# A fused attention and MLP block on one core: tile 0's value product in two column halves, tile 1's statistics on ScalarE, w2 loaded in two parts, and a new order of the work

## The chip, the core and the metric

The kernel runs on one core of a Trainium2 chip. The core has TensorE (PE, matrix products), VectorE (DVE), ScalarE (ACT), GpSimd (POOL) and SyncE (SP), which here only issues transfers; 16 DMA engines carry these. The metric is the device time of one execution in microseconds (us).

## The reference

The input x has 2048 tokens of 448 features. Two branches work on the same layernorm of x and are added to it:

```python
xn = _layernorm(x)
return x + _A_ref(xn, wqkv, w_phi, wo) + _B_ref(xn, w1, w2, w3, w4)

# _A_ref: linear attention, 16 heads of 28
pq = einsum("bhsd,hdf->bhsf", q, w_phi); pk = the same of k
phi_q = concat([softmax(pq), softmax(-pq)]); phi_k = the same of pk
kv = einsum("bhsf,bhsd->bhfd", phi_k, v); z = sum of phi_k over tokens
o = einsum(phi_q, kv) / (einsum(phi_q, z) + 1e-6); return o @ wo

# _B_ref: a mixer and an MLP
h = gelu(_layernorm(xn) @ w1)
hs = (four column groups of h, shifted by +1, -1, +2, -2 tokens) @ w2
x1 = xn + hs
return x1 + gelu(_layernorm(x1) @ w3) @ w4
```

## The kernel before, in words

The tokens are 16 tiles of 128 (NT = 16). Weights and activations are bf16, products accumulate in the 8 PSUM banks (`banks`). A class `Recorder` (lines 19 to 222) takes every operation in program order, works out which semaphore waits the data need, and plays each engine's list in that order; so the order of the Python calls is the order of every engine and of every DMA queue. Its helpers `mm` (L204), `tr` (L208), `act` (L212), `ew` (L216), `dma_t` (L219) and `dma` (L222) are the lines that the profile names.

TensorE is used as two halves of 64 rows that run at the same time: LO (rows 0 to 63) and HI (rows 64 to 127). The contraction over 448 features lies in four overlapping blocks of 128 (`lap`), so that a product is seven matmuls of 64 rows: four on one half and three on the other.

Two lists set the order. `chain([...], 400, "1001...")` plays the first stage; each entry makes a job:

- `HD` dummy products that keep TensorE busy; `L(("m", i))` the statistics of tile i on VectorE (`bn_stats`, `bn_aggr`, into `mv`); `("q", i, 1)` the reciprocal root on ScalarE and `("r", i, 1)` on GpSimd (into `rs`); `("a", i)` applies the layernorm on VectorE, `("p", i)` on GpSimd, into `xn`.
- `XT(i, ...)` transposes tile i on TensorE and copies it to `xnT`; `XD(i)` does it by a DMA transpose on SyncE.
- `ZV(i, EV(...))` the value product of tile i and its copy to `vaug`; `ZW`, `ZH` the product with w1 (whole, or 256 columns) and its gelu to `hT`; `ZR` the last 64 features of it (`rest_out` to gT, then `rest_T`, the DMA transpose hRT<-gT); `FO` folds w_phi into the weights of q and k (casts to `wpk`, `wpq`).
- `do(h_shift, g)` six DMA copies hT<-hT, which bring the shifted column groups to where the w2 product reads them with the HI rows (the LO rows read `hT` directly); `do(load_w2)`, `do(load_w3, h)` weight loads. All of these stand in SyncE's queue.
- `HF(p, n)` half n of the first head pair: p = 0 the first w2 product (tiles 0 and 1, reads `w2`, `hT` and `hRT`), p = 1 the k product, p = 2 the q product.

The string gives, for each "zip" job, which half takes four of the seven matmuls; 400 is the distance, in columns, that `chain` keeps between the halves' work on one bank. `vb` and `gb` name the PSUM bank of each value and w1 product. The second list, `play([...])`, orders the rest: k and q products and their exponentials (`k0`, `q0`), w2 products (`w0`, `w1_`), the second layernorm (`lo`, `sc`, `A` on GpSimd, `AD` on VectorE), k's norm (`kn`, `kx`), the sums over tokens (`K`), w3 and w4 products (`a`, `b`, `f`), the attention output (`N`) and stores (`S`).

Of the kernel before, what the change touches and what calls it, by code (L numbers as in the profile page):

```python
# [12 lines left out]
LN_EPS = 1e-5  # L13
# [211 lines left out]
def bass_parallel_sum__linear_kernel_hedgehog__mixer_s_mlp__prompt_kernel(  # L225
# [17 lines left out]
    with es:  # L243
# [172 lines left out]
        R.ew(pool, "memset", st[:, :, 8:9], D * LN_EPS)  # L416
        R.ew(dve, "memset", vp[:, :, DH + 1:VP], 0.0)
# [457 lines left out]
        def ln1(*ops):  # L875
            for op, *n in ops:
                if callable(op):
                    op()
                elif op == "m":
                    ln_stats(st, mv, xtok, *n)  # L880
                elif op == "r":
                    ln_scale(mv, rs, *n)
                elif op == "q":
                    ln_root(*n)
                elif op == "v":
                    ln_var(st, mv, *n)
                else:
                    ln1_apply(pool if op == "p" else dve, *n)
# [47 lines left out]
        def HF(p, n):  # L936
# [4 lines left out]
        vb = {0: 6, 1: 7, 2: 5, 3: 0, 4: 6, 5: 5, 6: 1, 7: 1, 8: 0, 9: 7, 10: 6, 11: 2, 12: 7, 13: 7, 14: 5, 15: 2}  # L941
        gb = ((4, 2, 3), (7, 6, 4), (3, 0, 5), (0, 5, 6))
        spin(30)
        chain([
            HD(1, 3), HD(3, 3), do(load_wT, 0, (1, 2, 3)), HD(2, 3), L(("m", 1)), L(("q", 1, 1)), L(("m", 0)),
            L(("q", 0, 1)), HD(3, 3), L(("a", 1)), L(("p", 0)), HD(5, 3), XT(1, 2, 1, "ACT"), HD(0, 3), L(("m", 2)),
            L(("m", 3)), XT(0, 2, 1, "ACT"), L(("q", 3, 1)), L(("r", 2, 1)), L(("m", 4)), L(("a", 3)), L(("q", 4, 1)),
            L(("m", 5)), ZV(1, EV(1, "ACT", 1)), ZV(0, EV(0, "ACT", 1)), L(("p", 2)), XT(2, 4, 1, "ACT"),
            inside(1, ZH(1, 0), XT(3, 0, 1, "ACT")), L(("m", 7)), L(("r", 5, 1)), L(("a", 4)), L(("p", 5)),
            L(("q", 7, 1)), L(("m", 6)), L(("r", 6, 1)), ZH(2, 0), L(("a", 7)), ZV(2, EV(2, "ACT", 1)),  # L950
            inside(1, ZH(0, 0), XT(4, 0, 1, "ACT")), L(("p", 6)), inside(2, ZH(0, 1, EW(0, 0, 1)), XT(5, 6, 1, "2")),
            L(("m", 15)), inside(1, ZH(2, 1), XT(7, 0, 1, "2")), L(("q", 15, 1)), L(("p", 15)),
            ZV(4, EV(4, "ACT", 1)), L(("m", 14)), inside(2, ZH(1, 1, EW(0, 1, 2)), XT(6, 0, 1, "DVE")), L(("m", 12)),
            ZV(5, EV(5, "ACT", 1)), L(("r", 14, 1)), L(("m", 13)), L(("p", 14)), ZV(6, EV(6, "ACT", 1)), L(("m", 11)),
            ZW(1, 0, EW(1, 0, 1)), ZW(1, 1, EW(1, 1, 1)), ZW(1, 2, EW(1, 2, 1)), L(("m", 10)), L(("r", 13, 1)),
            L(("r", 12, 1)), XT(14, 2, 2, "ACT"), L(("a", 12)), L(("r", 11, 1)), ZV(7, EV(7, "DVE", 1)), L(("a", 13)),
            L(("m", 8)), L(("p", 11)), ZV(3, EV(3, "ACT", 1)), ZV(15, EV(15, "ACT", 1)), XT(12, 6, 1, "2"),
            do(kv_picks), XT(13, 3, 1, "2"), do(phi_blocks), L(("r", 10, 1)), L(("r", 8, 1)), XD(11),
            L(("a", 10)), XD(10), ZV(14, EV(14, "ACT", 1)), L(("m", 9)), L(("p", 8)), ZV(12, EV(12, "DVE", 1)),
            ZW(3, 0, EW(3, 0, 1)), XT(8, 3, 1, "ACT"), FO(1, 2, 0), do(h_shift, 0), L(("r", 9, 1)),  # L960
            ZW(3, 2, EW(3, 2, 1)), FO(1, 0, 0), FO(1, 2, 1), ZV(13, EV(13, "ACT", 1)), ZW(3, 1, EW(3, 1, 1)),
            FO(1, 0, 1), L(("p", 9)), ZV(8, EV(8, "DVE", 1)),
            inside(3, ZR(0, 6, (rest_out, 0, 6), (rest_T, 0)), XT(9, 1, 1, "DVE")), FO(0, 0, 0), FO(0, 2, 0),
            ZR(1, 7, (rest_out, 1, 7)), do(load_w2), FO(0, 0, 1), ZW(2, 2, EW(2, 2, 1)), ZW(2, 1, EW(2, 1, 1)),
            FO(0, 2, 1), do(load_w3, 0), ZV(10, EV(10, "ACT", 1)), ZW(2, 0, EW(2, 0, 1)), do(rest_T, 1),
            ZV(9, EV(9, "ACT", 1)), ZV(11, EV(11, "DVE", 1)), HF(1, 0), HF(0, 0), HF(2, 0), HF(1, 1), do(late_3), do(kv_ones),
            HF(0, 1), HF(2, 1), do(h_shift, 1)], 400,
            "100100110101110000101010011110100")
# [62 lines left out]
        def wo_in(eng="SP"):  # L1031
# [4 lines left out]
            (lo, 1), (load_w3, 1), (k0, 1), (w0, 2), (lo, 0), (kn, 0), (k1, 1), (q0, 1), (w1_, 2), (q1, 1), (T, 0),  # L1036
            (k0, 2), (q0, 2), (k1, 2), (q1, 2), (k0, 3), (q0, 3), (T, 1), (kn, 1), (T, 3), (k1, 3), (w0, 4), (q1, 3),
            (kx, 0), (kn, 2), (T, 2), (kx, 1), (w1_, 4), (kn, 3), (k0, 4), (T, 5), (w0, 6), (k1, 4), (lo, 3), (kx, 2),
            (q0, 4), (lo, 2), (w1_, 6), (q1, 4), (kn, 4), (k0, 5), (kx, 3), (k0, 6), (sc, 0), (k1, 5), (w0, 8),
            (wo_in,), (q0, 5), (A, 0), (w1_, 8), (k1, 6), (T, 6), (AD, 1), (T, 4), (q0, 6), (kn, 5), (T, 7), (q1, 5),  # L1040
            (w0, 10), (load_w4, 0), (A, 3), (k0, 7), (A, 2), (w1_, 10), (q1, 6), (lo, 5), (lo, 6), (w0, 12), (k1, 7),
            (q0, 7), (G, 0), (K, 0), (kx, 4), (K, 1), (G, 1), (kx, 5), (lo, 7), (lo, 4), (G, 2), (K, 3), (K, 4),
            (G, 3), (sc, 4), (K, 6), (A, 7), (kn, 6), (K, 9), (q1, 7), (load_w4, 1), (A, 6), (A, 4), (w1_, 12),
            (K, 8), (K, 5), (K, 7), (lo, 10), (A, 5), (K, 11), (K, 2), (kx, 6), (G, 4), (kn, 7), (G, 7), (K, 10),
            (a, 0), (lo, 11), (kx, 7), (a, 1), (G, 6), (b, 0), (lo, 12), (b, 1), (w0, 14), (a, 2), (lo, 8), (a, 3),
# [48 lines left out]
```

## Time and profile before

| | before |
|---|---|
| runs | 170.62, 171.19, 171.85 us (median 171.19) |
| profiled execution | 171.11 us, of which the span of the trace is 169.4 us |
| TensorE busy | 165.0 us, 97% of the span, 2355 matmuls |
| VectorE, ScalarE, GpSimd busy | 109.9, 79.6 and 92.4 us |
| granted TensorE clock | 1.00 of full speed |
| chain that ended last | TensorE 86%, SyncE's queue 4%, DMA 4%, VectorE 3% |

A row of a timeline has the start in us, the duration in us, the engine (PE matmuls, PEld weight loads, SPq transfers being issued by SyncE), the line, the operation with its output and inputs, and in brackets the idle time ahead of it and what ended that. A row of busy time by stretch has the stretch, its length, the busy time of PE, PEld, DVE, ACT and POOL with the number of instructions in brackets, the granted clock, the share of the DMA engines and GB/s. The chain has start, duration, and what the time went to. A row of DMA issues has the count, the size of each and the median us from issue to landing.

### The profile page before, as it was taken

To read this page: it belongs to the slowest core of one execution; us is meant where nothing else is said; L and a number is where in the kernel's file an instruction comes from. 1 tells how busy PE (TensorE), PEld (TensorE's weight loads), DVE (VectorE), ACT (ScalarE), POOL (GpSimd) and SP (SyncE) were. 2 spreads that over 40 slices of the span, in tenths; PEclk is the share of its full clock that TensorE was granted. 3 is DMA by queue.
4 is the path that set the end of the run, shared out by engine and by line. 5 is a ranking of instruction groups with operands and counts; after the bars stand their busy time and mean duration, and the time that the engine had idled before them with its cause. 6 is when DMAs were issued, how large, how long until landed. Compare 5 with 4: busy or idle time off the path is not lost.

```text
span 169.4 us, 5416 instructions
## 1 busy us (share of the span) xinstructions
PE 165.0 (97%) x2355; PEld 99.2 (59%) x2355; DVE 109.9 (65%) x247; ACT 79.6 (47%) x107; POOL 92.4 (55%) x126
## 2 busy tenths in 40 slices
PE   8899999999999999999999999999999999999994
PEld 7476678666888775535554555545555555544453
DVE  2899777269999999995885836755755252560031
ACT  3489964849998787455242420440140222224000
POOL 5569872002999999994455684162362724252040
DMA  5995443799999976459785159363133112013021
GB/s 146 356 217 105 75 90 85 144 294 270 194 117 240 241 102 191 68 112 130 165 110 107 24 108 154 77 106 63 32 66 85 35 54 62 0 31 99 17 81 54
DMA packets 50583, 19.93 MB, mean 118 GB/s; under 512 B 41728, under 2 KB 49856, under 8 KB 50560
## 3 DMA queue, kind: packets, MB, share of 16 engines
q1 hardware_dynamic: 49440, 18.71, 55.1%
q10 hardware_dynamic: 1120, 0.89, 1.6%
q8 instruction: 18, 0.29, 0.8%
q14 instruction: 5, 0.04, 0.1%
HBM read 7.14 MB, written 1.84 MB: 53 GB/s over the span
## 4 chain that ended last, share of the span: by engine, by line
PE 86%; SPq 4%; DMA 4%; DVE 3%; POOL 1%; issue 1%
PE banks L204 85%; SPq L222 4%; DMA xtok<-in_A_x_dram 2%; DMA hRT<-gT 2%; DVE st L216 1%; PE banks L208 1%; DVE vaug L216 1%; POOL rs L216 1%; DVE mv L216 0%; POOL xn L216 0%; DVE xn L216 0%; SPq L219 0%
## 5 line engine op out<-in xcount | busy, mean ns | idle before, releaser
L212 ACT ACTIVATE phik<-banks 128x1024 bf16<-128x1024 f32 (+1 forms) x44 | 41.6, 987 | 63.5 <-PE banks L204 63.5
L204 PE MATMUL banks<-gT,w 64*128 64x512 bf16 x392 | 47.1, 376 | 0.1
L216 DVE TENSOR_TENSOR vaug<-banks,vaug 128x464 f32<-128x464 f32 (+3 forms) x65 | 32.8, 514 | 20.5 <-PE banks L204 18.8
L204 PE MATMUL banks<-w,phik 64*128 64x448 bf16 (+3 forms) x434 | 45.2, 343 | 0.0
L216 POOL TENSOR_TENSOR xnT<-vaug 128x280 bf16<-128x280 f32 (+1 forms) x32 | 18.1, 588 | 35.6 <-DVE vaug L216 35.6
L721 POOL TENSOR_TENSOR phik<-phik,rks 128x1792 bf16<-128x1792 bf16 x8 | 25.6, 3215 | 15.3 <-DVE rks L216 15.3
L204 PEld LDWEIGHTS banks<-w,phik 64*128 64x128 bf16 (+1 forms) x434 | 22.3, 94 | 19.5 <-issue 0.4
L204 PE MATMUL banks<-wv,xnT 64*128 64x448 bf16 (+2 forms) x222 | 33.0, 346 | 0.1
L204 PEld LDWEIGHTS banks<-gT,w 64*128 64x128 bf16 x392 | 18.3, 94 | 19.5 <-ACT phik L212 1.4
L216 POOL TENSOR_TENSOR vaug<-xn,xtok 128x448 f32<-128x448 bf16 x16 | 16.2, 1032 | 9.1 <-DVE vaug L216 9.1
L204 PEld LDWEIGHTS banks<-wv,xnT 64*128 64x128 bf16 (+1 forms) x222 | 13.7, 94 | 9.0 <-ACT xnT L212 0.8
L216 DVE RECIPROCAL vaug<-banks 128x16 f32<-128x16 f32 x16 | 4.1, 257 | 21.6 <-PE banks L204 21.6
L204 PE MATMUL banks<-xnT,w 64*128 64x512 bf16 (+1 forms) x105 | 17.6, 334 | 0.0
L216 DVE TENSOR_REDUCE ksum<-phik 128x64 f32<-128x1792 bf16 x8 | 16.0, 1997 | 0.2 <-ACT phik L212 0.2
L204 PE MATMUL banks<-wpk,xnT 64*128 64x448 bf16 x112 | 15.4, 349 | 0.0
L204 PE MATMUL banks<-wpq,xnT 64*128 64x448 bf16 x112 | 15.1, 349 | 0.0
L212 ACT ACTIVATE hi<-banks 128x896 bf16<-128x896 f32 x16 | 13.9, 937 | 1.2 <-PE banks L204 1.2
L204 PE MATMUL banks<-w,hT 64*128 64x448 bf16 x96 | 14.0, 349 | 0.0
L216 POOL TENSOR_TENSOR rs<-mv,mhalf 128x1 f32<-128x1 f32 (+1 forms) x14 | 9.6, 690 | 2.6 <-DVE mv L216 2.4
L216 POOL TENSOR_SCALAR g_tok<-xn,rs 128x512 bf16<-128x512 bf16 x12 | 9.2, 775 | 2.9 <-DMA gT<-g_tok 2.6
L204 PEld LDWEIGHTS banks<-wpk,xnT 64*128 64x128 bf16 x112 | 8.7, 94 | 2.6 <-ACT phik L212 0.2
L216 DVE BATCH_NORM_STATS2 st<-xtok 128x6 f32<-128x448 bf16 x16 | 9.7, 604 | 0.7 <-DMA xtok<-in_A_x_dram 0.7
(63 smaller groups left out, 167.2 us busy)
## 6 DMA issues: line engine op xcount, KB each, us to landing
w<-in_B_w_dram SPq DMA_DIRECT2D x2, 896.0 KB, 5.5
out_dram<-vaug SPq DMA_DIRECT2D x15, 112.0 KB, 1.9
w<-in_B_w_dram SPq DMA_DIRECT2D x2, 784.0 KB, 5.6
xtok<-in_A_x_dram SPq DMA_DIRECT2D x2, 448.0 KB, 6.5
wv<-in_A_wo_dram SPq DMA_DIRECT2D x2, 224.0 KB, 3.7
xtok<-in_A_x_dram SPq DMA_DIRECT2D x3, 112.0 KB, 4.0
xtok<-in_A_x_dram ACTq DMA_DIRECT2D x3, 112.0 KB, 4.2
w<-in_B_w_dram SPq DMA_DIRECT2D x1, 336.0 KB, 4.3
```

The source lines that it names most:

```text
L204: self.op("PE", lambda e: e.matmul(out, lhsT, rhs, start=start, stop=stop, skip_group_check=True), [out], [lhsT, rhs], tile=self._tile(lhsT))
L208: self.op("PE", lambda e: e.transpose(out, in_, ident), [out], [in_, ident], tile=self._tile(in_))
L212: self.op("ACT", lambda e: e.activation(out, in_, func, **kw), [out], [in_] + aps)
L216: self.op(eng, lambda e: getattr(e, name)(out, *args, **kw), [out], aps)
L222: self.op(eng, lambda e: e.dma_start(out, in_), [out], [in_], dma=True)
L721: R.op(pool, lambda e: e.tensor_tensor(ph, ph, wide, op=ALU.mult), [ph], [ph, wide, *after])
```

## The change

Four things are changed; what is computed stays.

1. The value product of tile 0 is made by `HC(0, 0)` and `HC(0, 1)`: two column halves of 224 in banks 0 and 1, of which LO begins with the first and HI with the second, and then they cross over. It is 14 matmuls of 224 columns instead of 7 of 448, and `EC` copies both banks with one ScalarE instruction.
2. The statistics of tile 1 come from ScalarE: `act_sum` runs twice over the tile (a copy scaled by -1/448 with an accumulated output, which is minus the mean, and a square with that as bias, whose accumulated output is the sum of squares), and `act_root` takes the root. VectorE loses one `bn_stats` and one `bn_aggr`, GpSimd gets a memset of the epsilon and applies tile 1.
3. `load_w2` is in two parts: first the two pieces of 64 rows, then the large piece.
4. Both lists, the string and the bank tables are new.

```diff
-        def load_w2(eng="SP"):
-            R.dma(w2[:, 0:NH, :], B_w2[0:REST, :].rearrange("(m p) d -> p m d", p=128), eng)
-            for h in range(2):
-                R.dma(w2[64 * h:64 * h + 64, NH, :], B_w2[REST:D, :], eng)
+        def load_w2(h, eng="SP"):
+            if h:
+                for k in range(2):
+                    R.dma(w2[64 * k:64 * k + 64, NH, :], B_w2[REST:D, :], eng)
+            else:
+                R.dma(w2[:, 0:NH, :], B_w2[0:REST, :].rearrange("(m p) d -> p m d", p=128), eng)
...
+        R.ew(pool, "memset", st[:, 1, 0:1], LN_EPS)
...
-            m, op = (mvt[:, i, 0:1], ALU.subtract) if eng == dve else (rst[:, i, 1:2], ALU.add)
+            m, op = (mvt[:, i, 0:1], ALU.subtract) if eng == dve and (mvt is mv2 or i != 1) else (rst[:, i, 1:2], ALU.add)
...
+        def act_sum(i, sq):
+            t, o = xn[:, NT - 1 - sq, 0:D], mv[:, i, 1:2] if sq else rs[:, i, 1:2]
+            m = rs[:, i, 1:2]
+            if sq:
+                R.op("ACT", lambda e: e.activation(t, xtok[:, i, :], ACT.Square, bias=m, accum_out=o), [t, o],
+                     [xtok[:, i, :], m])
+            else:
+                R.op("ACT", lambda e: e.activation(t, xtok[:, i, :], ACT.Copy, scale=-1.0 / D, accum_out=o), [t, o],
+                     [xtok[:, i, :]])
+
+        def act_root(i):
+            R.act(rs[:, i, 0:1], mv[:, i, 1:2], ACT.Abs_reciprocal_sqrt, scale=1.0 / D, bias=st[:, i, 0:1])
...
-            if eng == pool:
+            if eng == pool and i != 1:
                 ln_neg(mv, rs, i, 1)
...
+        def HC(i, n, *then):
+            v = lap_pair([banks[vb[i] + k][:, 0:D // 2] for k in range(2)],
+                         lambda k, kc, lo, hi: xnT[lo:hi, kc, 128 * i:128 * i + 128],
+                         lambda k, kc, lo, hi: wv[lo:hi, kc, D // 2 * k:D // 2 * k + D // 2], False)
+            return "both", halves_of(*v[n], n == 0), then
+
+        def EC(i):
+            vd = vaug[:, i, :].rearrange("p (b h e) -> p b h e", b=2, e=VP)[:, :, :, 0:DH]
+            vs = two(vb[i])[:, :, 0:D // 2].rearrange("p b (h e) -> p b h e", e=DH)
+            return R.act, vd, vs, ACT.Copy
...
-            HD(1, 3), HD(3, 3), do(load_wT, 0, (1, 2, 3)), HD(2, 3), L(("m", 1)), L(("q", 1, 1)), L(("m", 0)),
...
+            HD(3, 3), L(("m", 0)), HD(0, 3), L(("s", 1, 0)), HD(2, 3), L(("q", 0, 1)), L(("s", 1, 1)), L(("t", 1)),
...
-            ZR(1, 7, (rest_out, 1, 7)), do(load_w2), FO(0, 0, 1), ZW(2, 2, EW(2, 2, 1)), ZW(2, 1, EW(2, 1, 1)),
...
+            XD(10), do(load_w2, 1), FO(1, 2, 1), ZW(3, 1, EW(3, 1, 1)), L(("p", 9)), do(load_w2, 0), do(h_shift, 0),
...
```

What this makes of SyncE's queue between the last weight transposes (hi<-in_A_wqkv) and w3, first before (x6 and the like mean that so many equal rows follow one another; xnT<-xn are `XD(11)` and `XD(10)`, the hT<-hT rows `h_shift(0)`, the first hRT<-gT `rest_T(0)`):

```order
L219 DMA_TRANSPOSE xnT<-xn 128x4x128 x2
L222 DMA hT<-hT 48x1024
L222 DMA hT<-hT 32x1023
L222 DMA hT<-hT 16x1024
L222 DMA hT<-hT 16x1023
L222 DMA hT<-hT 32x1024
L222 DMA hT<-hT 48x1022
L222 DMA w2<-in_B_w2_dram 128x3x448
L222 DMA w2<-in_B_w2_dram 64x448 x2
L219 DMA_TRANSPOSE hRT<-gT 128x4x128
L222 DMA w3<-in_B_w3_dram 128x2x1792
```

and after:

```order
L219 DMA_TRANSPOSE xnT<-xn 128x4x128 x2
L222 DMA w2<-in_B_w2_dram 64x448 x2
L222 DMA w2<-in_B_w2_dram 128x3x448
L222 DMA hT<-hT 48x1024
L222 DMA hT<-hT 32x1023
L222 DMA hT<-hT 16x1024
L222 DMA hT<-hT 16x1023
L222 DMA hT<-hT 32x1024
L222 DMA hT<-hT 48x1022
L219 DMA_TRANSPOSE hRT<-gT 128x4x128
L222 DMA w3<-in_B_w3_dram 128x2x1792
```

The three loads of w2 have moved ahead of the six shift copies; hRT<-gT follows all nine in both.

VectorE's list around the apply of tile 10 (TENSOR_SCALAR xn<-xtok,mv,rs), which the second xnT<-xn transpose reads; before:

```order
L216 CAST vaug<-banks 128x16x28
L216 COPY xnT<-banks 128x4x64
L216 MEMSET pick 32x1 x4
L216 COPY xnT<-banks 128x4x64
L216 TENSOR_TENSOR g_tok<-g_tok,maskb 112x448
L216 TENSOR_SCALAR xn<-xtok,mv,rs 128x512
```

and after, where the first TENSOR_SCALAR is tile 11 and the second tile 10:

```order
L216 TENSOR_SCALAR xn<-xtok,mv,rs 128x512
L216 CAST vaug<-banks 128x16x28
L216 TENSOR_SCALAR xn<-xtok,mv,rs 128x512
L216 TENSOR_TENSOR g_tok<-g_tok,maskb 112x448
L216 CAST vaug<-banks 128x16x28
```

Tile 10's apply now stands ahead of the masking of g_tok, and the copies and memsets have gone behind it; tile 11's apply has come from GpSimd.

TensorE's first products, before (L208 rows are transposes of a tile, eight each; 128x448 and 128x256 are a matmul's columns; `wv,xnT` is a value product, `xnT,w1` a w1 product):

```order
L208 MATMUL banks<-ident,xn 128x64 x8
L204 MATMUL banks<-const-bfloat16-1.0 128x128 x6
L208 MATMUL banks<-ident,xn 128x64 x8
L204 MATMUL banks<-wv,xnT 128x448 x10
L208 MATMUL banks<-ident,xn 128x64 x8
L204 MATMUL banks<-xnT,w1 128x256
```

and after:

```order
L208 MATMUL banks<-ident,xn 128x64 x8
L204 MATMUL banks<-const-bfloat16-1.0 128x128 x6
L208 MATMUL banks<-ident,xn 128x64 x8
L204 MATMUL banks<-wv,xnT 128x224 x14
L204 MATMUL banks<-wv,xnT 128x448 x3
L208 MATMUL banks<-ident,xn 128x64 x8
L204 MATMUL banks<-xnT,w1 128x256
```

Ten matmuls of 448 columns ahead of tile 2's transposes have become fourteen of 224 and three of 448. The first transposes are of tile 1 before and of tile 0 after.

More of the change, by code (lines that the diff above doesn't have):

```diff
@@ new lines, in bass_parallel_sum__linear_kernel_hedgehog__mixer_s_mlp__prompt_kernel @@
+            ZV(2, EV(2, "ACT", 1)), L(("m", 6)), L(("r", 6, 1)), L(("a", 7)), inside(1, ZH(0, 0), XT(4, 0, 1, "ACT")),
+            inside(2, ZH(0, 1, EW(0, 0, 1)), XT(5, 6, 1, "2")), inside(1, ZH(2, 1), XT(7, 0, 1, "ACT")), L(("m", 14)),
+            L(("p", 6)), do(load_wT, 0, (1, 2, 3)), L(("r", 14, 1)), L(("m", 15)), L(("p", 14)),
+            ZV(4, EV(4, "DVE", 1)), inside(2, ZH(1, 1, EW(0, 1, 2)), XT(6, 0, 1, "DVE")), L(("m", 12)),
+            ZV(5, EV(5, "ACT", 1)), L(("r", 15, 1)), L(("r", 12, 1)), ZW(1, 2, EW(1, 2, 1)), L(("p", 12)),
@@ new lines, in bass_parallel_sum__linear_kernel_hedgehog__mixer_s_mlp__prompt_kernel @@
+            ZW(1, 1, EW(1, 1, 1)), ZV(3, EV(3, "ACT", 1)), L(("a", 15)), L(("m", 13)), XT(14, 2, 2, "ACT"),
+            L(("m", 11)), L(("m", 9)), L(("r", 13, 1)), L(("m", 8)), ZW(1, 0, EW(1, 0, 1)), L(("m", 10)),
+            L(("p", 13)), L(("r", 11, 1)), ZV(6, EV(6, "DVE", 1)), L(("a", 11)), ZV(14, EV(14, "ACT", 1)),
+            L(("r", 8, 1)), ZV(15, EV(15, "DVE", 1)), XD(11), L(("r", 10, 1)), L(("a", 10)), XT(12, 6, 1, "ACT"),
+            do(phi_blocks), XT(13, 3, 1, "ACT"), L(("p", 8)), ZV(7, EV(7, "ACT", 1)), ZV(12, EV(12, "DVE", 1)),
@@ new lines, in bass_parallel_sum__linear_kernel_hedgehog__mixer_s_mlp__prompt_kernel @@
+            L(("r", 9, 1)), ZW(3, 0, EW(3, 0, 1)), XT(8, 4, 1, "2"), ZW(3, 2, EW(3, 2, 1)), FO(1, 2, 0), FO(1, 0, 0),
+            XD(10), do(load_w2, 1), FO(1, 2, 1), ZW(3, 1, EW(3, 1, 1)), L(("p", 9)), do(load_w2, 0), do(h_shift, 0),
+            FO(1, 0, 1), ZV(13, EV(13, "ACT", 1)), ZV(8, EV(8, "ACT", 1)),
+            inside(3, ZR(0, 6, (rest_out, 0, 6), (rest_T, 0)), XT(9, 3, 1, "DVE")), do(late_3), FO(0, 2, 0),
+            FO(0, 0, 0), ZW(2, 0, EW(2, 0, 1)), ZW(2, 2, EW(2, 2, 1)), ZW(2, 1, EW(2, 1, 1)), do(kv_ones),
@@ L970, in bass_parallel_sum__linear_kernel_hedgehog__mixer_s_mlp__prompt_kernel @@
+            FO(0, 2, 1), ZV(9, EV(9, "ACT", 1)), do(kv_picks), ZV(11, EV(11, "ACT", 1)), do(load_w3, 0), FO(0, 0, 1),
+            ZR(1, 1, (rest_out, 1, 1)), ZV(10, EV(10, "DVE", 1)), HF(1, 0), HF(0, 0), do(rest_T, 1), do(h_shift, 1),
+            HF(2, 0), HF(1, 1), HF(0, 1), HF(2, 1)], 400,
+            "11101010111001010001010011110010")
         kp = [phi_pair(wpk, 2 * n, kq[n][0]) for n in range(8)]
@@ L1041, in bass_parallel_sum__linear_kernel_hedgehog__mixer_s_mlp__prompt_kernel @@
[L1041 to L1045, printed above, removed]
```

79 lines of the change are left out of this document (34 added, 45 removed).

## The prediction

> **What bounds the kernel now.** I read the page first, then busy time by stretch, then the chain of waits in order of time, then the timelines of single engines at the places that the chain names. The page's first line and the stretches say where time can be won at all:
>
> ```profile
> PE 165.0 (97%) x2355; PEld 99.2 (59%) x2355; DVE 109.9 (65%) x247; ACT 79.6 (47%) x107; POOL 92.4 (55%) x126
> ```
> ```profile
> 4.00:8.00 4.00, 3.19 (x61) 1.90 (x61) 3.45 (x11) 1.69 (x5) 2.06 (x5) 1.00 1.08 353
> 8.00:12.00 4.00, 3.91 (x82) 2.69 (x78) 3.63 (x12) 3.08 (x9) 2.73 (x6) 1.00 1.64 273
> 32.00:36.00 4.00, 3.77 (x40) 2.09 (x41) 0.85 (x5) 2.40 (x3) 0.00 (x0) 1.00 0.80 223
> ```
>
> TensorE is the bound, at full granted clock (the 1.00 behind the counts). Its matmul work is the same after the change (below), so a new order can only remove idle TensorE time, and there is little: after 8 us only the stretch from 32 us is visibly short. The chain names what ended last in the first third:
>
> ```profile
> 1.71 4.04 DMA xtok<-in_A_x_dram
> 5.77 0.64 DVE st L216
> 10.50 0.78 POOL xn L216
> 11.33 0.29 PE banks L208 x8
> 27.01 0.59 SPq L222
> 30.12 2.72 DMA hRT<-gT
> 32.97 32.65 PE banks L204 x513
> 65.72 101.35 PE banks L204 x1269
> ```
>
> Up to 5.77 us the kernel waits for x; around 11 us for a normalized tile; then for SyncE's queue and the transpose hRT<-gT, up to 32.97; from there TensorE runs through. So two places can change: the start and the first w2 product.
>
> **The change, part by part.** Term 1, the first w2 product. SyncE's queue and TensorE there:
>
> ```profile
> 19.52 3.49 SPq L219 DMA_TRANSPOSE xnT<-xn  x2
> 23.06 4.55 SPq L222 DMA_DIRECT2D hT<-hT  x6
> 27.65 2.43 SPq L222 DMA_DIRECT2D w<-in_B_w_dram  x3
> 30.12 1.27 SPq L219 DMA_TRANSPOSE hRT<-gT  x1
> ```
> ```profile
> 21.36 1.66 SPq L219 DMA_TRANSPOSE xnT<-xn  x1
> ```
> ```profile
> 20.92 0.41 DVE L216 TENSOR_SCALAR xn<-xtok,mv,rs 128x512 bf16<-128x512 bf16 x1
> ```
> ```profile
> 31.96 0.09 PEld L204 LDWEIGHTS banks<-w,hT 64*128 64x128 bf16 x1 [0.26 <-DMA w<-in_B_w_dram]
> ```
> ```profile
> 31.97 0.36 PE L204 MATMUL banks<-w,hT 64*128 64x448 bf16 x1
> 32.17 0.35 PE L204 MATMUL banks<-w,hT 64*128 64x448 bf16 x1
> 32.20 0.35 PE L204 MATMUL banks<-wv,xnT 64*128 64x448 bf16 x1
> 32.36 0.35 PE L204 MATMUL banks<-w,hT 64*128 64x448 bf16 x1
> 32.40 0.35 PE L204 MATMUL banks<-wv,xnT 64*128 64x448 bf16 x1
> 32.97 0.35 PE L204 MATMUL banks<-w,hRT 64*128 64x448 bf16 x1 [0.23 <-DMA hRT<-gT]
> 32.98 0.36 PE L204 MATMUL banks<-wv,xnT 64*128 64x448 bf16 x1
> ```
>
> Each row half of TensorE starts a 448-column product every 0.19 to 0.20 us (31.97, 32.17, 32.36). The next on the first half, which reads hRT, comes at 32.97 instead of 32.36 + 0.19 = 32.55: 0.42 us lost. The other half loses as much (32.40 to 32.98, less 0.19 = 0.39), since its product stands behind the waiting one. The first weights of w2 cost a wait too: 0.26 us of no weight load, of which the first half feels some and the other half, busy with the value product, none; I count at most 0.14. In all about 0.4 to 0.5 us; the bounds are 0.23 (both halves idle, the row at 32.97) and 0.42 + 0.26 = 0.68 (all of both).
>
> The change issues w2's three transfers ahead of the six shift copies. The queue is in order and all ten instructions stay, so the hRT transpose still follows six copies and three loads; what moves it is that the second xnT<-xn transpose no longer waits. The first, at hRT's 1.27, ends at 19.52 + 1.27 = 20.79; the second begins at 21.36, when VectorE has just made xn[10] (20.92 + 0.41 = 21.33): 0.58 us idle. After the change that apply stands earlier in VectorE's list, ahead of the masking of g_tok, the copies of xnT and four memsets that are before it now; by my walk through the list it is done at 20.2 to 20.4 us, ahead of 20.79. So hRT is issued at 30.12 - 0.58 = 29.54 and lands, with the same 2.72, at 32.26. TensorE wants it at about 32.4 to 32.5 (the 32.55 above, less what it did not lose on w2). Then the wait is gone: -0.44 us. If xn[10] comes later than 20.79, hRT follows one for one; above 0.4 us late nothing of the gain is left.
>
> What is late next: the shift copies, now behind 448 KB of w2. The sixth was issued at 27.01 and must be so at 27.01 + 2.43 + 0.04 - 0.58 = 28.90. It is read only by the other half's third w2 product, 0.77 us behind the hRT product's place (first one below, then 0.19 each), so near 33.3 us. That leaves 4.4 us to land.
>
> ```profile
> 33.37 0.35 PE L204 MATMUL banks<-w,hT 64*128 64x448 bf16 x1
> ```
> ```profile
> w<-in_B_w_dram SPq DMA_DIRECT2D x1, 336.0 KB, 4.3
> hT<-hT SPq DMA_DIRECT2D x2, 32.0 KB, 3.8
> hT<-hT SPq DMA_DIRECT2D x1, 95.9 KB, 5.5
> hT<-hT SPq DMA_DIRECT2D x1, 31.9 KB, 5.2
> ```
>
> Shift copies took 3.8 to 5.5 us from issue to landing; most are under 4.4, so I cost this at nothing and keep 5.5 - 4.4 = 1.1 us for the range. w2 itself, issued from about 22.5 us, needs 4.3 us and is read near 31.9: covered by 5 us.
>
> Term 2, the start. TensorE's early work and what holds it:
>
> ```profile
> 3.52 0.63 DVE L216 BATCH_NORM_STATS2 st<-xtok 128x6 f32<-128x448 bf16 x1 [0.38 <-DMA xtok<-in_A_x_dram]
> 5.77 0.63 DVE L216 BATCH_NORM_STATS2 st<-xtok 128x6 f32<-128x448 bf16 x1 [0.31 <-DMA xtok<-in_A_x_dram]
> ```
> ```profile
> 6.71 0.57 POOL L216 TENSOR_TENSOR rs<-mv,mhalf 128x1 f32<-128x1 f32 x1
> 7.66 0.77 POOL L216 TENSOR_SCALAR xn<-xtok,rs 128x512 bf16<-128x512 bf16 x1
> ```
> ```profile
> 8.48 0.17 PEld L208 LDWEIGHTS banks<-ident,xn 64*128 64x128 bf16 x8 [0.38 <-POOL xn L216]
> ```
> ```profile
> 6.75 1.80 PE L204 MATMUL banks<-wv,xnT 64*128 64x448 bf16 x10
> ```
> ```profile
> 4.47 0.20 ACT L212 ACTIVATE rs<-mv 128x1 f32<-128x1 f32 x1 [2.40 <-DVE mv L216]
> 9.79 0.55 ACT L212 ACTIVATE vaug<-banks 128x448 bf16<-128x448 f32 x1
> ```
>
> Before the transposes of tile 2 at 8.48 TensorE has only tiles 0 and 1: ten value products of 448 columns from 6.75. The change puts fourteen of 224 (seven times 448) and three of 448 there: the same columns, also ten. And tile 2 hangs on its own x (5.77), its statistics, and POOL's three steps from 6.71 to 7.66 + 0.77 = 8.43, which the change leaves. Whatever tiles 0 and 1 win ends in that wait. VectorE's freed 0.63 (and an aggregate of 0.2) falls in its idle time ahead of 5.77. The two passes of tile 1's statistics on ScalarE have no row; the nearest is 0.55 for 128x448, so 1.1 us, 1.5 if each cost the 0.20 of a 128x1 more. From 3.5 us with tile 0's root (0.20) between, they end at 4.9 to 5.3; POOL, which applied tile 0 ahead of it, applies tile 1 by 6.1, still before it is wanted at 6.71. Nothing, then; twice the upper price would push POOL by 1 us and with it tile 2 (+0.5). The Trainium skill (ScalarE: Activation LUTs, What ACT_TABLE_LOAD costs) gives an ACTIVATE 186 ns + 0.833 ns per element, and 93 ns for each pointer operand. By it the two are an estimated 0.56 + 0.65 = 1.2 us; the same page's Rules for kernel authors give such arithmetic to VectorE, and if tile 1 were what TensorE waits for, the move would by these figures cost 1.2 - 0.8 = 0.4 us and the sum be 171.1. The trace agrees on the durations (0.63 and an aggregate against about 1.1) and not on the cost, since ScalarE idles 2.40 us ahead of 4.47.
>
> Past 8.5 us the later gates move by tenths both ways: tile 5's transposes waited for POOL until 11.33 (the chain's row) and now come an apply earlier, but tile 7's copy is whole on ScalarE, 0.60 instead of 0.38, ahead of tile 6's. I take -0.05, bounds -0.3 and +0.3.
>
> Term 3, all else: more second-layernorm applies on VectorE (65% busy) and fewer on POOL, wo's loads earlier, w4's halves swapped. The chain's longest rows are TensorE alone (32.65 + 101.35 us), and the moved consumers keep at least 0.2 us by my walk: 0, bounds -0.2 and +0.5.
>
> Sum: -0.44 - 0.05 + 0 = -0.5 us. The profiled execution took 171.11 us (span 169.4, 1.7 around it), 0.08 under the median of the runs shown. I forecast 170.7 us.
>
> **Rivals.** A: no gain, 171.1. The hRT transpose moves 0.58 at most and needs about 0.4 of it; xn[10] 0.4 late, a slower transpose (the second hRT transpose took 6.4 us, row below), or the cast of wpq on VectorE just ahead of the same product would hold TensorE up to the old time. For it: the margin is 0.15 to 0.3 us. Against: fewer bytes are in flight beside hRT now. That is also the case in which the change doesn't do what its order suggests.
>
> ```profile
> DMA to landing us min/median/max: 2.7/4.5/6.4
> ```
>
> B: a larger gain from the start, 169.3 to 170.0. TensorE loses 0.81 us in 4 to 8 us and 0.09 in 8 to 12. If the statistics on ScalarE and the crossing halves fed it without a gap, up to 0.9 more would come off 170.6. Against: the gate at 8.48 stands on x's landing.
>
> C: slower, 171.9. The shift copies land late behind w2. The place is the other half's w2 products from 33.37 on; the price is 1.1 us at a landing of 5.5, and it decides from 4.4 us upward; 170.65 + 1.1 = 171.75, and 171.9 if the following copies shift too. For it: rows of 5.2 and 5.5. The Trainium skill (DMA: Bandwidth & Descriptors, Issuing engines are not separate DMA queues) has all transfers share 16 engines and interleave, so w2's bytes cost the copies bandwidth wherever they stand; the DMA share of 0.80 in 32 to 36 us says that it is thin here. Against: w2, issued from 22.5 us and 4.3 us in flight, has landed by about 28.5, before the last copies are issued.
>
> **How the numbers follow.** Forecast 0.42, A 0.25, B 0.13, C 0.20 (with what my walk may have overlooked in term 3). The forecast's own range is 170.2 to 171.0. With A (to 171.4), half of B (down to 169.5) and most of C (up to 172.3) the range is 169.5 to 172.3. Within 1% (about what a measurement of this kernel can tell from no change) is 169.5 to 172.9: the forecast, A, half of B and over half of C, 0.82. Faster by over 1%: half of B, 0.07. Slower by over 1%: half of C, where several copies are late or another wait joins it, 0.11.
>
> **What would show it.** Right: no idle time ahead of the second xnT<-xn, hRT issued near 29.5 and landed by 32.4, the hRT product 0.19 us behind its neighbour, the stretch 32 to 36 near 4.00 busy, and tile 2's transposes still near 8.5. Wrong: the hRT product still waits (A), tile 2's transposes before 8.2 (B), the other half's w2 products waiting for DMA hT (C), or any idle stretch of TensorE beyond 36 us.

## The result, and the profile after

The changed kernel takes 172.34 us (median of 21 runs, 171.31 to 174.53) against 171.01 us (21 runs) for the kernel before: a ratio of 1.0073, with a 95% interval of 1.0054 to 1.0091. It is slower by 0.7%, 1.3 us; I had forecast 170.7 us. Its profiled execution took 171.70 us, with a span of 170.0 us.

The chain of waits of the changed kernel (start, duration, what) is the first thing to read. It shows that the wait that the forecast was about is gone, and where more than the gain was lost:

```profile
8.57 0.29 PE banks L208 x8
...
25.43 21.52 PE banks L204 x316
...
61.67 4.52 DMA gT<-g_tok
66.19 0.14 issue
66.32 101.35 PE banks L204 x1268
```

The waits for hRT near 30 us are gone from the chain. New in it is a transpose gT<-g_tok, 4.52 us from issue to landing. Behind it stand the same 101.35 us of TensorE as before, but they start at 66.32 instead of 65.72. Those 0.6 us are the whole difference of the two spans (170.0 and 169.4). The medians differ by more, 1.3 us: the profiled execution was the third fastest of the changed kernel's 21.

Busy time by stretch, first the kernel before and then the changed one (PE busy is the third number):

```profile
64.00:68.00 4.00, 3.90 (x126) 2.32 (x124) 3.94 (x6) 3.01 (x3) 3.81 (x6) 1.00 0.71 203
```
```profile
32.00:36.00 4.00, 4.00 (x52) 3.02 (x47) 1.37 (x3) 2.06 (x3) 0.00 (x0) 1.00 1.37 266
64.00:68.00 4.00, 2.38 (x104) 1.53 (x90) 3.97 (x5) 2.31 (x3) 3.63 (x6) 1.00 0.71 209
```

The stretch from 32 us is full now (3.77 before). The one from 64 us has lost 1.52 us of TensorE.

**The first w2 product.** SyncE's queue and TensorE's first half in the changed kernel:

```profile
19.52 2.72 SPq L219 DMA_TRANSPOSE xnT<-xn  x2
22.29 2.35 SPq L222 DMA_DIRECT2D w<-in_B_w_dram  x3
24.70 4.69 SPq L222 DMA_DIRECT2D hT<-hT  x6
29.43 1.29 SPq L219 DMA_TRANSPOSE hRT<-gT  x1
```
```profile
31.68 0.35 PE L204 MATMUL banks<-w,hT 64*128 64x448 bf16 x1
31.87 0.35 PE L204 MATMUL banks<-w,hT 64*128 64x448 bf16 x1
32.06 0.36 PE L204 MATMUL banks<-w,hRT 64*128 64x448 bf16 x1
```

The two xnT<-xn transposes take 2.72 us instead of 3.49, hRT is issued at 29.43 (I had said 29.54), and the hRT product follows its neighbour after 0.19 us. The work that TensorE has done ahead of this product is the same in both kernels (23.8 us, counted from the matmuls' columns, dummies left out, at the 0.19 us per 448 columns of the rows above, with both halves at once), so its start can be compared: 32.97 before, 32.06 now, 0.91 us earlier. Of this 0.45 was there before the w2 product, and 0.46 comes from the waits that went. The margin was thin: hRT landed at 32.02, 0.04 us ahead of its product.

**The first w3 product.** SyncE's queue from the second half of w3 to the second part of w4, before and after (of each pair of w rows the first is w3 and the second w4; wv is wo's buffer):

```profile
37.20 0.59 SPq L222 DMA_DIRECT2D w<-in_B_w_dram  x1
39.96 7.85 SPq L219 DMA_TRANSPOSE eqT_lo<-hi  x5
47.86 2.13 SPq L222 DMA_DIRECT2D wv<-in_A_wo_dram  x2
50.03 4.31 SPq L219 DMA_TRANSPOSE eqT_lo<-hi  x3
54.38 0.58 SPq L222 DMA_DIRECT2D w<-in_B_w_dram  x1
56.88 6.00 SPq L219 DMA_TRANSPOSE gT<-g_tok  x4
```
```profile
38.46 1.13 SPq L222 DMA_DIRECT2D wv<-in_A_wo_dram  x2
39.63 0.47 SPq L222 DMA_DIRECT2D w<-in_B_w_dram  x1
40.14 16.20 SPq L219 DMA_TRANSPOSE eqT_lo<-hi  x8
56.39 0.58 SPq L222 DMA_DIRECT2D w<-in_B_w_dram  x1
57.02 5.93 SPq L219 DMA_TRANSPOSE gT<-g_tok  x4
```

The first row of eqT transposes in the changed kernel holds one that took 5.87 us to issue:

```profile
41.43 5.87 SPq L219 DMA_TRANSPOSE eqT_lo<-hi  x1
```

The gT transposes are issued at nearly the same time (56.88 and 57.02). What differs is w4, 784 KB, just ahead of them: issued at 54.38 before and at 56.39 now. In the landing events of the trace the four transposes come at 60.3, 62.3, 62.8 and 64.1 before, and at 63.2, 63.7, 64.2 and 66.2 now, the first of them 6.2 us after its issue instead of 3.4. TensorE now wants them earlier, and waits (the last rows of its timeline at this place):

```profile
63.75 0.95 PE L204 MATMUL banks<-phik,vaug 128*30 128x64 bf16 x96
66.32 1.90 PE L204 MATMUL banks<-gT,w 64*128 64x512 bf16 x16 [1.62 <-DMA gT<-g_tok]
```

### The profile page after: what moved, and what is told of

The parts are those of the page before. It is cut to its first block, busy times and chain, and to the rows that moved or that the text cites. A ratio compares the mean times of both kernels' runs of the same rounds, so it can differ in the third digit from the quotient of the medians.

```text
span 170.0 us, 5428 instructions
## 1 busy us (share of the span) xinstructions
PE 164.2 (97%) x2362; PEld 101.3 (60%) x2362; DVE 109.6 (64%) x247; ACT 81.3 (48%) x110; POOL 90.6 (53%) x125
## 4 chain that ended last, share of the span: by engine, by line
PE 82%; POOL 7%; DMA 5%; DVE 3%; SPq 1%; issue 1%
PE banks L204 81%; POOL phik L737 4%; DMA gT<-g_tok 3%; DMA xtok<-in_A_x_dram 2%; POOL g_tok L216 1%; POOL rs L216 1%; DVE ksum L216 1%; PE banks L208 1%; DVE xn L216 1%; SPq L219 0%; SPq L222 0%; POOL xn L216 0%; DVE st L216 0%; DVE rks L216 0%; DVE vaug L216 0%
## 5 line engine op out<-in xcount | busy, mean ns | idle before, releaser
L212 ACT ACTIVATE phik<-banks 128x1024 bf16<-128x1024 f32 (+1 forms) x44 | 41.2, 988 | 63.8 <-PE banks L204 63.7
L204 PE MATMUL banks<-gT,w 64*128 64x512 bf16 x392 | 46.5, 376 | 1.6 <-DMA gT<-g_tok 1.6
L204 PE MATMUL banks<-wv,xnT 64*128 64x448 bf16 (+5 forms) x229 | 32.6, 341 | 0.1
L204 PE MATMUL banks<-xnT,w 64*128 64x512 bf16 (+1 forms) x105 | 16.3, 334 | 0.0
L216 DVE TENSOR_TENSOR xn<-banks,xn 128x512 bf16<-128x512 f32 (+1 forms) x16 | 8.9, 599 | 3.2 <-PE banks L204 3.2
L204 PEld LDWEIGHTS banks<-wpk,xnT 64*128 64x128 bf16 x112 | 9.3, 94 | 1.9
L216 DVE BATCH_NORM_STATS2 st<-xtok 128x6 f32<-128x448 bf16 x15 | 9.0, 598 | 1.8 <-DMA xtok<-in_A_x_dram 1.8
```

The costliest lines, as they stand in the source:

```text
L204: self.op("PE", lambda e: e.matmul(out, lhsT, rhs, start=start, stop=stop, skip_group_check=True), [out], [lhsT, rhs], tile=self._tile(lhsT))
L212: self.op("ACT", lambda e: e.activation(out, in_, func, **kw), [out], [in_] + aps)
L216: self.op(eng, lambda e: getattr(e, name)(out, *args, **kw), [out], aps)
```

## The experiments

Each ratio is to runs of the kernel before on the same chip. "TensorE on equal work" below compares start times at the same amount of columns done, as above.

### What makes the new wait

`w4_behind_g` moves one load of w4 behind the first four gT transposes:

```diff
-            (q0, 7), (lo, 5), (T, 6), (load_w4, 1), (lo, 6), (K, 0), ...
+            (q0, 7), (lo, 5), (T, 6), (lo, 6), (K, 0), ...
-            (K, 9), (G, 2), (K, 10), ...
+            (K, 9), (G, 2), (load_w4, 1), (K, 10), ...
```

> The changed kernel with one load of w4 moved in SyncE's queue from ahead of the first four gT transposes to behind them. Theory 1 (TensorE waits 1.6 us near 64.7 because 784 KB of w4, issued at 56.4, are in flight ahead of the gT transposes, which then take 4 to 6 us instead of 2.5): the last of the four lands by 64.0, the wait at the first w3 product is under 0.2 us, and the time is 170.2 us, about 2 us under the changed kernel's 172.3 and 0.8 under the kernel before. Theory 2 (the transposes are late because SyncE issues them late or GpSimd makes g_tok late): they are issued within 0.7 us of where they were, the wait stays over 1 us, and the time stays near 172.

`wo_back` puts the loads of wo back to their old place, and leaves w4:

```diff
-            (lo, 1), (lo, 0), (wo_in,), (k0, 1), (load_w3, 1), ...
+            (lo, 1), (lo, 0), (k0, 1), (load_w3, 1), ...
-            (w0, 8), (k1, 6), (kn, 4), ...
+            (w0, 8), (wo_in,), (k1, 6), (kn, 4), ...
```

> The changed kernel with the two loads of wo put back to their place of before, behind w3's second half and four of the eqT transposes. Theory 1, with the early wo loads as the reason why w4 is issued 2 us later than before (w3's second half at 39.6 instead of 37.2, its landing at 47.4, and the eqT transpose that is held until then): w3 lands by 44.5, w4 is issued by 54.8, lands by 60, the gT transposes land by 64.2, the wait is under 0.3 us and the time 170.3. A rival (the order of the eqT transposes or the swapped halves of w4 make the loss, wo has no part in it): w4 is still issued after 56, and the time stays near 172.

`both_back` has both edits:

> The changed kernel with both edits: wo's loads put back and the w4 load behind the four gT transposes. If both act on the same wait, this is no better than either alone: 170.2 us, within 0.2 of them. If they act on two waits, it is faster than the better one by over 0.5 us.

`w4_twice` instead moves the other load of w4 up as well, directly behind the first:

```diff
-            (q0, 7), (lo, 5), (T, 6), (load_w4, 1), (lo, 6), ...
+            (q0, 7), (lo, 5), (T, 6), (load_w4, 1), (load_w4, 0), (lo, 6), ...
-            (b, 0), (lo, 8), (b, 1), (load_w4, 0), (lo, 9), ...
+            (b, 0), (lo, 8), (b, 1), (lo, 9), ...
```

> The changed kernel with the second load of w4 moved up as well, so that 1568 KB instead of 784 KB stand ahead of the gT transposes. Theory 1 (bytes in flight ahead of the transposes set their landing): they land 4 to 5 us later than in the changed kernel, the wait at the first w3 product grows from 1.6 to about 6 us, and the time is 176 to 177 us. Theory 2 (late issue alone): one more issue of 0.6 us, the wait grows by that, and the time is 172.9 us.

Measured: w4_behind_g 170.99 us (ratio to the kernel before 0.9992, interval 0.9963 to 1.0020), wo_back 170.99 (0.9993, 0.9964 to 1.0022), both_back 171.06 (1.0004, 0.9974 to 1.0033), w4_twice 175.30 (1.0223, 1.0174 to 1.0272). Either edit alone takes the changed kernel's 1.3 us off, and both together no more: they act on one wait. (The absolute times, forecast at 170.2 to 170.3, were missed; the last section of the experiments takes this up.) In wo_back the queue runs nearly as in the kernel before, and the first w3 product starts without a wait:

```profile
38.33 0.59 SPq L222 DMA_DIRECT2D w<-in_B_w_dram  x1
...
54.48 0.59 SPq L222 DMA_DIRECT2D w<-in_B_w_dram  x1
56.15 6.53 SPq L219 DMA_TRANSPOSE gT<-g_tok  x4
```
```profile
65.00 3.20 PE L204 MATMUL banks<-gT,w 64*128 64x512 bf16 x28
```

In w4_behind_g the last of the four is issued at 61.6, as in the changed kernel (61.7), and lands at 64.1 instead of 66.2: not its issue was late but its transfer.

```profile
56.33 6.50 SPq L219 DMA_TRANSPOSE gT<-g_tok  x4
62.87 1.20 SPq L222 DMA_DIRECT2D w<-in_B_w_dram  x2
```

In w4_twice the wait grows from 1.62 to 3.75 us:

```profile
68.29 4.02 PE L204 MATMUL banks<-gT,w 64*128 64x512 bf16 x20 [3.75 <-DMA gT<-g_tok]
```

The first of the four landed 2.0 us later than in the changed kernel (65.2 instead of 63.2), directly behind the second load of w4 (64.8). So bytes of w4 ahead of the transposes set when they land. The size was off: I expected 6 us of wait, from a whole transfer more, and the last transpose landed 1.9 us later (68.1 instead of 66.2). It did so because it was issued later, at 63.51 instead of 61.67: the other load took 0.6 us to issue, and two of the transposes 2.34 and 2.19 us instead of 1.29 and 1.26. From issue to landing it took as long as in the changed kernel (4.54 and 4.52 us). So this run doesn't separate w4's bytes from late issue for the last transpose; w4_behind_g does. The time went up by 3.0 us rather than 2.1; the 1269 products behind the wait took 103.04 us there instead of 101.35, at a granted clock of 0.99. (The one execution of w4_twice at a clock of 1.00 took 174.02 us, 1.7 over the changed kernel's median.)

The bytes of w4 alone don't make 1.62 us, though. Each transfer has 16 landing events in the trace. Of the changed kernel's last gT transpose 15 had come by 64.63, and TensorE, whose product ahead ended at 64.70, would hardly have waited for that. The sixteenth came at 66.19. In between lies a packet of a queue that the DMA view lists apart from the kernel's transfers, with 18 packets of 16 KB (0.29 MB, 0.8% of the DMA engines' span):

```profile
q8 instruction: 18, 0.29, 0.8%
```

One of these packets ran from 64.01 to 65.13 us. Of the transpose's 32 last packets, of 4 bytes each, 30 had begun by 64.02; the other two begin at 65.12 and 65.13, as the 16 KB packet ends. In the kernel before and in w4_behind_g, wo_back and both_back the transpose was through before that packet began, by about 0.3 us in the closest two (in w4_behind_g by 63.69, the packet began at 63.97), and landed whole. So, in this profile, w4 cost the transpose about half a microsecond (15 parts by 64.63, against all 16 by 64.05 in w4_behind_g, issued 0.1 us apart) and with it the margin, and the packet seems to have made 1.6 us of wait out of that. In w4_twice such a packet (65.04 to 66.15) falls into the second transpose, of which one part landed at 65.66 and 15 at 66.98 or later. This is read from packets and not tested by an experiment, and it is one profile; the medians, 1.3 us apart, say that a loss of this order is no exception.

Why w4 came late: w3's second half moved from 37.20 to 39.63, 1.13 us of it by the early wo loads and the rest by shift copies that end later. It also took longer to land, 7.8 us from issue instead of 5.6 (5.4 in wo_back), with the 448 KB of wo issued just ahead of it. Then the second eqT transpose was held in its issue, from 41.43 to 47.30, up to 0.1 us ahead of w3's landing at 47.4. (In w4_behind_g, w4_twice and wo_back the second eqT transpose is held as well, and let go 0.1 to 0.2 us ahead of w3's landing.) With the wo loads out of there (wo_back) w3 goes out at 38.33, lands at 43.8, and w4 goes out at 54.48, though the shift copies are still late. So the two ends of the chain, the wo loads and w4 ahead of gT, are each shown by an experiment; the held transpose between them is read from the trace.

### The first w2 product

`w2_back` (on wo_back) returns w2's loads to their place behind the shift copies, with the early transpose kept:

```diff
-            XD(10), do(load_w2, 1), FO(1, 2, 1), ..., do(load_w2, 0), do(h_shift, 0),
+            XD(10), FO(1, 2, 1), ..., do(h_shift, 0), do(load_w2, 0), do(load_w2, 1),
```

> Base: the kernel with wo's loads put back (170.99 us, profiled span 168.7). Here the loads of w2 also go back behind the six shift copies, with the second xnT<-xn transpose still early. My first term said that the gain at the first w2 product comes from that transpose, which no longer holds SyncE's queue, and not from the order of w2: then hRT lands by 32.3 as in the base, w2 is issued near 27 and lands by 31.4, TensorE waits for neither, and the span stays within 0.2 of 168.7. The rival, that the order of w2 does it: the first w2 product waits for w2 or hRT for 0.3 us or more, and TensorE's time at that place is that much later.

`before_a10` (on before_x12, below) has nothing of the change but an earlier apply of tile 10:

```diff
-            ... XT(12, 6, 1, "2"), do(kv_picks), XT(13, 3, 1, "2"), do(phi_blocks), L(("r", 10, 1)), ..., L(("a", 10)), XD(10),
+            ... L(("r", 10, 1)), XT(12, 6, 1, "2"), L(("a", 10)), do(kv_picks), XT(13, 3, 1, "2"), do(phi_blocks), ..., XD(10),
```

> before_x12 with one apply moved: tile 10's, which the second xnT<-xn transpose reads, stands ahead of the memsets, the copy of tile 13 and the masking of g_tok on VectorE. Nothing else of the change is in it; w2 stays behind the shift copies. By my first term SyncE's queue then no longer waits 0.58 us, w2 lands by 31.6 and hRT by 32.3, the wait at the first w2 product falls from 0.44 us to under 0.1, and the time is 0.4 us under before_x12. The rival, that w2's place ahead of the copies is needed: the first w2 product still waits for w2 or hRT for 0.3 us or more.

Measured: w2_back 170.58 us (0.9977, 0.9945 to 1.0008); before_a10 171.11 (0.9987, 0.9966 to 1.0008). TensorE at the first w2 product, first w2_back, then before_a10, then before_x12, which has the old order:

```profile
32.61 0.35 PE L204 MATMUL banks<-w,hT 64*128 64x448 bf16 x1
...
32.80 0.35 PE L204 MATMUL banks<-w,hRT 64*128 64x448 bf16 x1
```
```profile
33.04 0.35 PE L204 MATMUL banks<-w,hT 64*128 64x448 bf16 x1
...
33.23 0.35 PE L204 MATMUL banks<-w,hRT 64*128 64x448 bf16 x1
```
```profile
32.51 0.35 PE L204 MATMUL banks<-w,hT 64*128 64x448 bf16 x1
...
33.51 0.35 PE L204 MATMUL banks<-w,hRT 64*128 64x448 bf16 x1 [0.64 <-DMA hRT<-gT]
```

With the transpose early there is no wait, wherever w2 stands (0.19 us from one row to the next); without it the hRT product is 1.00 us behind, 0.81 too much. The stronger of the two runs is before_a10, where hRT landed at 31.97, 0.87 us earlier than in the kernel before, with w2 in its old place. In w2_back hRT landed at 32.65, only 0.15 ahead of its product, and TensorE came 0.7 us later than in wo_back, after a late landing of x; its span was 169.4 us and not within 0.2 of 168.7 as expected. So the gain at this place comes from the apply of tile 10 and not from the order of w2. In before_a10 it was spent on the spot: the moved apply took 0.86 us on VectorE instead of 0.41 and delayed the copy of tile 13 behind it, and TensorE on equal work fell 0.5 us back against before_x12 between 20 and 22 us. What doubled that apply was not tried; GpSimd is at work on xn[8] then.

```profile
20.36 0.86 DVE L216 TENSOR_SCALAR xn<-xtok,mv,rs 128x512 bf16<-128x512 bf16 x1
```

### The start

`stats_dve` (on wo_back) returns tile 1's statistics to VectorE:

```diff
-            if eng == pool and i != 1:
+            if eng == pool:
...
-            HD(3, 3), L(("m", 0)), HD(0, 3), L(("s", 1, 0)), HD(2, 3), L(("q", 0, 1)), L(("s", 1, 1)), L(("t", 1)),
+            HD(3, 3), L(("m", 0)), HD(0, 3), L(("m", 1)), HD(2, 3), L(("q", 0, 1)), L(("q", 1, 1)),
```

> Base: wo's loads put back. Here tile 1's statistics go back to VectorE (bn_stats, bn_aggr, the negative mean on GpSimd); the order stays. In the changed kernel TensorE reached its work at 13 to 32 us 0.24 to 0.47 us earlier than in the kernel before. If the statistics on ScalarE made that, TensorE is 0.3 us or more later from 13 us on; if the order made it (tiles 5, 7 and 6 normalized earlier), TensorE is within 0.1 us of the base at 13 us and after.

`one_bank` (on wo_back) makes tile 0's value product one product of 448 columns, `one_bank4` (on x12_first) the same in bank 4:

```diff
-            HC(0, 0), HC(0, 1, EC(0)),
+            ZV(0, EV(0, "ACT", 1)),
-            "11101010111001010001010011110010")
+            "011101010111001010001010011110010")
```

> Base: wo's loads put back. Here tile 0's value product is a plain one of seven matmuls of 448 columns in one bank. By my second term it falls in the wait for tile 2 (near 8.5 us) and costs nothing: TensorE is within 0.1 us of the base from tile 2's transposes on. The rival, that the crossing halves gain: TensorE is 0.2 us or more later at 9 us and at 20 us.

> x12_first with tile 0's value product as one product of 448 columns, this time in bank 4. In bank 0 the same edit cost 1.2 us, and the wait stood at tile 3's transposes, which use banks 0 and 1, for ScalarE's copy of tile 0. If the bank made that loss, TensorE is here within 0.2 us of x12_first from tile 3's transposes on, and the time within 0.3. If the crossing halves themselves are worth something, the loss of 0.8 to 1.2 us stays.

stats_dve: 171.25 us (0.9990, 0.9962 to 1.0018). Up to 11.8 us TensorE, on equal work, is within 0.1 us of wo_back, so the statistics on ScalarE brought nothing and cost nothing. Behind that it lost 1.4 us, to a transfer that has nothing to do with the edit:

```profile
13.19 0.63 DVE L216 BATCH_NORM_STATS2 st<-xtok 128x6 f32<-128x448 bf16 x1 [1.50 <-DMA xtok<-in_A_x_dram]
```

one_bank: 172.22 us (1.0051, 1.0030 to 1.0072), one_bank4: 171.71 us (1.0025, 1.0001 to 1.0050). In one_bank TensorE stands at tile 3's transposes, which write banks 0 and 1, until ScalarE has emptied bank 0:

```profile
9.95 0.17 PEld L208 LDWEIGHTS banks<-ident,xn 64*128 64x128 bf16 x8 [1.13 <-ACT vaug L212]
```

In bank 4 that wait is gone and TensorE is within 0.3 us of x12_first up to 12 us, as the wait for tile 2 would have it; but it falls 0.6 us behind by 23 us and 1.2 by 37 us, much of it in waits for ScalarE's gelu (0.9 us). With another job at its head `chain` interleaves all later jobs otherwise, so this doesn't price the crossing halves by themselves. It shows that in this order they are not free to undo: my expectation of 0.3 us was wrong, and the 0.45 us gained by 31 us belong to the order with them, not to one edit that I could single out.

### Where the gain went in the median

The repaired kernels' profiles lie under the kernel before by what was forecast (wo_back 170.42, both_back 170.38 us against 171.11, 0.7 us), their medians don't. `before_look` is the kernel before once more, `x12_first` (on wo_back) and `before_x12` (on the kernel before) swap two loads of x:

```diff
-        load_x(8, 4)
-        load_x(12, 4)
+        load_x(12, 4)
+        load_x(8, 4)
```

> The kernel before, unchanged, for a second profile. If the waits of the first w2 product (0.4 us, for hRT) and of the start belong to the kernel, they are here again within 0.15 us; if they differ from execution to execution, this profile shows another lag at 13 us or at 33 us, and a part of the changed kernel's 0.85 us at 33 us is chance.

> The changed kernel with wo's loads put back, and x's tiles 12 to 15 loaded ahead of 8 to 11. In two profiles of the experiments before this one VectorE stood 0.5 and 1.5 us in its statistics of tile 14 until the last load of x had landed (12.4 and 13.2 us instead of 11.1), with the copy of tile 6 behind it, and TensorE waited. If these late landings make the median of the repaired kernel (170.99) lie above its fastest runs (170.2), the median falls to 170.5 or less and the wait is not in the profile. The rival, that the spread has another cause: the median stays at 171.0.

> The kernel before with the same swap of the two loads of x. Its VectorE takes tile 15's statistics at 11.9 us, 0.8 us after the landing of 11.1, so it has a little more room than the changed kernel (0.4 us). If late landings cost it as well, its median falls by 0.2 to 0.4 us, to 170.7; if they hit only the changed kernel, it stays at 171.0.

> x12_first again, for another profile. In its profile TensorE's time at 32 us was 0.4 to 0.5 us under that of the kernel before and its span 0.3 to 0.7 us under, but its median is the same. If late transfers at the start (x, or the weights of v and w1) take that gain in half of the executions, a profile with a time over 171 us has its extra idle time of TensorE before 20 us, ended by a transfer or by a chain that begins with one. If the gain is lost later, the extra idle time stands at the first w2 product, at the first w3 product or behind them.

`look2` to `look4` repeat it:

> The same kernel and the same question as in look1: a time over 171 us goes with idle time of TensorE before 20 us (late transfers at the start), or with idle time later.

> The same kernel and the same question as in look1: a time over 171 us goes with idle time of TensorE before 20 us (late transfers at the start), or with idle time later.

> The same kernel and the same question as in look1: a time over 171 us goes with idle time of TensorE before 20 us (late transfers at the start), or with idle time later.

before_look, 170.76 us, has the wait for hRT again: its products start at 31.94, 32.13 and 32.76, 0.44 us late. In before_x12 (171.26 us, 0.9997, 0.9975 to 1.0018) it was 0.81. So it belongs to the kernel. x12_first took 171.18 us (1.0001, 0.9972 to 1.0029): the swap narrowed nothing, and the late landing of tiles 12 to 15 isn't what holds the median. The four further profiles of it took 170.81, 170.12, 171.24 and 170.54 us. The slowest and the fastest differ at the start, in the statistics of tile 2, here in look3 and in look2:

```profile
6.35 0.63 DVE L216 BATCH_NORM_STATS2 st<-xtok 128x6 f32<-128x448 bf16 x1 [2.10 <-DMA xtok<-in_A_x_dram]
```
```profile
5.57 0.63 DVE L216 BATCH_NORM_STATS2 st<-xtok 128x6 f32<-128x448 bf16 x1 [1.28 <-DMA xtok<-in_A_x_dram]
```

Tile 2's x landed 0.8 us later in look3, TensorE is 0.8 us later at tile 2's transposes, and it is 0.6 us later from 10 to 60 us on equal work. In look1 and look3 another 0.5 us or so goes between 64 and 71 us, in idle time that no event of another engine ends. In both, and in one_bank4, it stands ahead of the 1110th matmul of the trace, and this begins 1.3 to 1.4 us after the end of a 16 KB packet of q8 that came late: it ended at 65.72 in look1 and the matmul began at 67.12. In look2, look4 and x12_first the packet began at 63.3 to 63.4, in look1 at 64.67 and in look3 at 64.95. That the packet causes the idle time is not shown. The late landing of x is chance that the kernel before can meet too; the idle time at the 1110th matmul stands in none of the four profiles with the old order (before, before_look, before_x12, before_a10), which are too few to say that it can't. So this explains the spread and only perhaps a part of why the medians agree, and that stays open: the profiles put the repaired kernels at a mean of 170.6 us (nine profiles of w4_behind_g, wo_back, both_back, w2_back and x12_first, 170.12 to 171.24) against 171.11 and 170.76 for the kernel before, the timed medians at 170.6 to 171.2 against 171.0 to 171.2, and the intervals of about 0.3% hold both no gain and the 0.5 us that I forecast, or most of it.

## Why the prediction was wrong

- **Term 1, the first w2 product: right in the trace.** Forecast -0.44 us, measured 0.46 in one profile. The mechanism is the one named (the apply of tile 10, and SyncE not waiting); w2's new place had no part in it. The margin that I put at 0.15 to 0.3 us was 0.04, since TensorE came 0.45 us earlier than I had it.
- **Term 2, the start: right in its gate, too small in its sum.** Tile 2's transposes stayed at 8.57 (8.49 before), behind the landing of x, and the statistics on ScalarE were neutral (their two passes took 0.58 and 0.65 us, and 0.2 each for reading the sums). But by the first w2 product the changed order was 0.45 us ahead, where I had taken -0.05 with bounds of -0.3 and +0.3: gates of tenths that I let cancel did not. Of the ten profiles with this start (five of them with x's loads swapped) nine are 0.35 to 0.65 us ahead of the kernel before at this place, and look3 is level with it.
- **Term 3, all else: this step failed.** I listed "wo's loads earlier, w4's halves swapped" and costed them at 0, with +0.5 as the upper bound, for no more reason than that "the moved consumers keep at least 0.2 us by my walk". They cost 1.62 us of waiting in the profile, and taking either back gives 1.3 us in the median. The walk gave no price to what is in flight: in the kernel before w4 had been issued 2 us earlier and landed at 59.6, and the last gT transpose, issued at 61.6, took 2.5 us. Moving 448 KB of wo ahead of w3 delayed w3, then the eqT transposes, then w4, and w4's bytes then stood in the way of the transposes that follow it. The last of these lost its margin by that, and in the profile a 16 KB packet of q8 seems to have held it up further. The prediction had named idle time of TensorE beyond 36 us as a sign of being wrong, and this is where it came.
- **The sum.** Even with Term 3 repaired the forecast 0.5 us stands in the profiles alone; the medians of the repaired kernels show no gain that their intervals can tell from nothing.
- **Rival C** had the right kind of mechanism, small transfers late behind a weight load, at the wrong place: the shift copies landed in time, and TensorE's other half took its w2 products without a wait. Its price of 1.1 us was near the true one only by chance. My sum set no such price on the queue past 37 us; only C's chance of 0.20 had room for "what my walk may have overlooked in term 3".
- **Rival A** and **rival B** did not hold: the wait for hRT went, and the start's gain was under half a microsecond, with the gate at 8.5 us in place.

## What to carry to other kernels

When a change moves loads in a queue that also carries small transfers on the critical path, cost each small transfer by what is in flight ahead of it at that moment, not by its latency in the old trace: follow the queue to its end, one displaced load after the other, until a stretch of idle queue time has taken up the shift. A margin of some tenths is little: here a packet that the kernel doesn't issue seems to have turned half a microsecond of lateness into 1.6. A gain early in a chain also moves every later reader forward, so the margin of each later transfer shrinks by the gain (here 0.9 us) before anything else is moved. And where a planner or a list interleaves the work, undoing one entry is another order, so price such an edit by the wait that it moves and not by the time of the whole.

## What the runs showed of the hardware

- A gT transpose with 784 KB issued 0.6 us ahead of it (the changed kernel) landed 6.2 us after its issue, and 3.4 us when the 784 KB were 2.5 us ahead (the kernel before); with none directly ahead the last of four took 2.5 us (w4_behind_g). They landed only behind w4: w4 at 61.2 and the first transpose at 61.8 in wo_back, 64.8 and 65.2 in w4_twice. The Trainium skill (DMA: Bandwidth & Descriptors, Two DMAs through the same engine are not ordered) says that within one queue of an engine descriptors start in order; these landings agree with it.
- The issue of a DMA transpose on SyncE can itself be held: 5.87 us (41.43 to 47.30), ending 0.1 us ahead of the landing of the 896 KB issued ahead of it; 5.82 and 5.85 us in w4_behind_g and w4_twice, again 0.1 us ahead of that landing, and 3.02 in wo_back, 0.2 ahead of it.
- The last load of x landed between 10.8 and 13.2 us, and tile 2's between 5.5 and 6.3, from one execution to the next, with the same queue ahead.
- One of the 16 parts of a small transfer can land over a microsecond behind the others: 66.19 against 64.63 for the changed kernel's last gT transpose, with a 16 KB packet of the queue q8 from 64.01 to 65.13; 60.05 against 58.48 for the first in both_back, with such a packet from 58.03 to 58.95; 62.74 against 61.21 for the second in before_a10, from 60.69 to 61.61.
